# Converting 64-bit weights while the first tokens are computed: seven blocks' low parts through accumulating transfers, and a new order of the start

## The chip, the cores and the metric

The kernel runs on one core of a Trainium2 chip. The metric is the device time of one execution in microseconds (us). Three runs of the kernel before took 881.94, 882.14 and 883.23 us, median 882.14. The engines are named as the profile names them: PE (TensorE, matrix products; PEld is its loading of the fixed operand), DVE (VectorE), ACT (ScalarE), POOL (GpSimd) and SP (SyncE, which here only issues transfers).

## The reference, cut to what matters

Attention in chunks of 64 positions, then a normalised two-layer FFN with a residual:

```python
scores = 0.125 * q_chunk @ k_chunk.T            # 8 x 8 heads, 9 chunks of 64 x 64 each
attn = exp(scores - max(scores)); attn /= sum(attn) + 1e-9
x = (attn @ v_chunk)                            # heads side by side: 4608 tokens x 512
xn = (x - mean) / sqrt(var + 1e-6) * g_ln
out = x + relu(xn @ w_ch1) @ w_ch2              # 512 -> 2048 -> 512
```

q, k, v and g_ln are 32-bit floats. The two weight matrices come out of the set-up as 64-bit floats, since a 32-bit array is multiplied by a 64-bit scalar there, and the kernel takes them as they are.

## The kernel before

**Tiling.** The 4608 tokens are 18 pairs of 256 tokens (PAIR); two pairs make a tile of 512, so there are nine tiles. The hidden layer is cut into 16 blocks f of 128. For block f the FFN does an *up* product (512 to 128, line 369) into a PSUM tile h, a *rectification* (`split`, lines 377 and 378: ACT writes the high part hh, DVE the rest hl) and *down* products (128 to 512, line 389) that accumulate in the sums y. Every operand is kept as a high part and a rest ("low part"), both in the format F32R, and each product is three matmuls: high x high, high x low, low x high. With three matmuls for each of four k-slices, an up product is 12 matmuls; the down products of one block are 6 matmuls for a single pair and 12 for a tile.

**Attention of one pair** (`attention`): load q_t and k_t (one buffer each), scores on PE (line 206), maximum and subtraction on DVE (213, 219), load v_t, exponential on ACT (223), transposition of the probabilities, product with v on PE (271), division by the row sums (x, line 286 or 294), statistics (304), xg (309), transposition of xg and its splitting into xth and xtl. For the first four pairs (by_pe) both transpositions are done by PE against an identity (231, 321), and the rest xtl is made by PE too: the product of xth with minus the identity (328) is added to the transposed x in PSUM. For the first two pairs (den_by_pe) the row sums are PE products as well (275). All these PE transpositions, the scores and x of these pairs use one PSUM tile of two banks, `banks()`, of which there is one. The later pairs are transposed on DVE (242, 339).

**Conversion of the weights** (`convert_w`). There are 17 units: units 0 and 1 are the two halves of block 0 (512 columns each), unit i from 2 on is block i - 1 (1024 columns: 512 of w1, 512 of w2). A unit goes through these steps: *fetch* (SP, line 104) of the 64-bit words into raw, *start* (ACT, 112: absolute value of the upper words into wf), *round* (DVE, 119, 120, 123: clamp, shift, merge with the lower words; the result is written over the lower words inside raw, at a stride of 8 bytes), *sign* (DVE, 129, in place; then ACT, 133, casts the result to the high part wh), *split* (the low part wl = value - wh). The split of units 0 to 3 (BY_PE = 4) is two matmuls on PE in the first sum bank of pair 1 or its neighbour (144, 145: identity x value minus wh), copied out by ACT (146); that of the others is a DVE subtraction (148). There is one buffer wf and there are three for raw; two of these lie where later blocks' weights will stand.

**Order.** Nothing is ordered by a planner: the program is emitted under `tc.manual_schedule()`, and each engine and each queue takes its instructions in the order in which they are emitted. `play` walks a string; each letter advances one generator to its next `yield`. In START, a, b, A, B and E are the attention of pairs 0, 1, 2, 3 and 4, w the conversion, u and v the products of pairs 0 and 1 for the blocks 0 to 5 (SINGLE = 6), 1 and 2 their rectifications, y and 3 products and rectifications of the whole tile 0 for the blocks 6 to 15. STEADY is played seven times, for tiles 1 to 7, and LAST for tile 8. In a step of w that starts unit i + 1, the split of unit i - 1 and the fetch of unit i + 2 are emitted too.

Of the kernel before, what the change touches and what calls it, by code (L numbers as in the profile page):

```python
# [23 lines left out]
NPAIR = T // PAIR  # L24
NTILE = NPAIR // 2
HP = H // 2
NK = DM // P
NF = DFF // P
NW = 2 * DM
# [2 lines left out]

START = "aawwwwaawwwwwwawbwawwawbwbabwwaawaaawwbwwuA1wbbu1uwuwuAuB1Awubu1u1Awbwuu1bbbbuwvwAvw22AwAAvvvvB2EwA2wvv2vABvy2w3yBvwAww3vAyAwwywwyw3yA3BwyBwByByByBw3wB3wyByBww3yyBwwyEw3wywyy33yy3"
STEADY = "ABu1Au1AuAu1AuAu1AuABuAu1AEu1AuAu1AuAu1AuAu1BuBu1BuBu1BuBu1BuBEuBBu1BBu1BuBBu1Buu1uu1"
LAST = "u1u1uu1uu1uu1uu1uu1uu1uu1uu1uu1uu1uu1uu1uu1uu1u1"

SINGLE = 6

BY_PE = 4

ROOM = (3, 11)

# [9 lines left out]
def chunk_attention_ffn(ctx: ExitStack, tc: tile.TileContext, qkv, g, w, out):  # L54
    nc = tc.nc
    PSUM = bass.MemoryType.PSUM

    const = ctx.enter_context(tc.tile_pool(name="const", bufs=1))
# [6 lines left out]
    raws = ctx.enter_context(tc.tile_pool(name="raws", bufs=1))  # L65
# [4 lines left out]
    ident = const.tile([P, P], F32, name="ident")  # L70
    make_identity(nc, ident)
    minus = const.tile([P, P], F32R, name="minus")
    nc.scalar.activation(minus, ident, AF.Copy, scale=-1.0)
    ones = const.tile([P, 2], F32, name="ones")
    nc.gpsimd.memset(ones, 1.0)
    mhalf = const.tile([P, 2], F32, name="mhalf")
# [8 lines left out]
    def weights(f):  # L85
        if f not in wp:
            wp[f] = const.tile([P, 2, NW], F32R, name="wp", tag=f"w{f}")
        return wp[f][:, 0, :], wp[f][:, 1, :]

    def part(i):  # L90

        return (0, slice(i * HALF, (i + 1) * HALF)) if i < 2 else (i - 1, slice(0, NW))

    units = NF + 1
    stage, converted = {}, set()

    def fetch_w(i):
        if i < units:
# [6 lines left out]
            words = raw.bitcast(U32).rearrange("p (n two) -> p n two", two=2)  # L105
            stage[i] = words[:, :, 0], words[:, :, 1]

    def start_w(i):
        if i < units:
            lo, hi = stage[i]  # L110
            wf = raws.tile([P, NW], F32, name="wf")[:, : lo.shape[1]]
            nc.scalar.activation(wf, hi.bitcast(F32), AF.Abs)  # L112
            stage[i] = lo, hi, wf

    def round_w(i):

        lo, hi, wf = stage[i]
        wu = wf.bitcast(U32)
        nc.vector.tensor_scalar(out=wf, in0=wf, scalar1=F64_LOW, scalar2=F64_HIGH, op0=ALU.max, op1=ALU.min)
        nc.vector.tensor_scalar(  # L120
            out=wu, in0=wu, scalar1=0x07FFFFFF, scalar2=3, op0=ALU.bitwise_and, op1=ALU.logical_shift_left
        )
        nc.vector.scalar_tensor_tensor(  # L123
            out=lo, in0=lo, scalar=29, in1=wu, op0=ALU.logical_shift_right, op1=ALU.bitwise_or
        )

    def sign_w(i):
        lo, hi, _ = stage[i]
        nc.vector.scalar_tensor_tensor(
            out=lo, in0=hi, scalar=0xC0000000, in1=lo, op0=ALU.bitwise_and, op1=ALU.bitwise_or  # L130
        )
        f, cs = part(i)
        nc.scalar.copy(weights(f)[0][:, cs], lo.bitcast(F32))

    def split_w(i):
        wf = stage.pop(i)[0].bitcast(F32)
        f, cs = part(i)
        wh, wl = (x[:, cs] for x in weights(f))
        if i < BY_PE:
            for j in range(wf.shape[1] // HALF):  # L140
                js = slice(j * HALF, (j + 1) * HALF)
                assert 1 not in taken
                z = sums(1)[j % 2]
                nc.tensor.matmul(z, lhsT=ident, rhs=wf[:, js], start=True, stop=False)  # L144
                nc.tensor.matmul(z, lhsT=minus, rhs=wh[:, js], start=False, stop=True)
                nc.scalar.copy(wl[:, js], z)
        else:
            nc.vector.tensor_tensor(out=wl, in0=wf, in1=wh.bitcast(F32), op=ALU.subtract)
        converted.update((0, i) if i < 2 else (2 * i - 2, 2 * i - 1))

    def convert_w():

        fetch_w(0)
        yield
        start_w(0)
        for i in range(1, 4):
            fetch_w(i)
            yield
        for i in range(units):
            round_w(i)  # L160
# [12 lines left out]
    ys, taken = {}, set()

    def sums(pair):

        if pair not in ys:
            ys[pair] = [ps_y.tile([P, DM], F32, name="y") for _ in range(2)]
        return ys[pair]

    def attention(pair, xt_cols, xs, by_pe, den_by_pe):
# [7 lines left out]
        scale = 1.0 / float(D) ** 0.5  # L189
        groups = 2 * HP  # L190

        def banks():
            return ps_a.tile([P, 2, DM], F32, name="s")

        def rows(bank):
            return bank.rearrange("p (a d) -> p a d", d=D)

        s2 = banks()
        s = [rows(s2[:, h2, :]) for h2 in range(2)]
        for j in range(2):  # L200
            for a in range(HP):
                for h2 in range(2):
                    r = slice(h2 * D, (h2 + 1) * D)
                    for c in range(2):
                        cs = slice(j * P + c * D, j * P + (c + 1) * D)
# [20 lines left out]

        pt_sb = work.tile([P, groups, 2, D], F32, name="pt_sb", tag="work")
        if by_pe:
            pt = banks().rearrange("p j (a t) -> p j a t", a=HP)
            for a in range(groups):  # L230
                nc.tensor.transpose(out=pt[:, a // HP, a % HP, :], in_=p_sb[:, a, :, :], identity=ident)  # L231
            for j in range(2):
                nc.scalar.copy(
                    pt_sb[:, j * HP : (j + 1) * HP], pt[:, j].rearrange("p a (c t) -> p a c t", c=2)
                )
            yield
        else:
            for h2 in range(2):
                for j in range(2):
                    for c in range(2):  # L240
                        for i in range(2):
                            nc.vector.transpose(  # L242
                                out=pt_sb[quad(2 * h2 + j), :, c, quad(i)], in_=p_sb[quad(2 * c + i), :, h2, quad(j)]
                            )
                    yield
# [67 lines left out]

        xth, xtl = xt_cols()
        if by_pe:
            xt = banks()
            for j in range(2):
                js = slice(j * P, (j + 1) * P)
                for k in range(NK):
                    ks = slice(k * P, (k + 1) * P)  # L320
                    nc.tensor.matmul(  # L321
                        xt[:, j, ks], lhsT=xg[:, j, ks], rhs=ident, is_transpose=True, start=k == 0, stop=k == NK - 1
                    )
                nc.scalar.copy(xth[:, :, js], xt[:, j, :].rearrange("p (k t) -> p k t", k=NK))  # L324
                yield
            for j in range(2):
                js = slice(j * P, (j + 1) * P)
                nc.tensor.matmul(  # L328
                    xt[:, j, :], lhsT=minus, rhs=xth[:, :, js], start=False, stop=True, skip_group_check=True
                )  # L330
                nc.scalar.copy(xtl[:, :, js], xt[:, j, :].rearrange("p (k t) -> p k t", k=NK))  # L331
                if j == 0:
                    yield
        else:
            xt = work.tile([P, 2 * NK, P], F32, name="xt", tag="work")
            xg = xg.rearrange("p j (k t) -> p (j k) t", k=NK)
            for j in range(4):
                for i in range(4):
                    nc.vector.transpose(out=xt[quad(j), :, quad(i)], in_=xg[quad(i), :, quad(j)])  # L339
                yield  # L340
            for j in range(2):
                js = slice(j * P, (j + 1) * P)
                xt_j = xt[:, j * NK : (j + 1) * NK, :]
                nc.scalar.copy(xth[:, :, js], xt_j)  # L344
                nc.gpsimd.tensor_tensor(out=xtl[:, :, js], in0=xt_j, in1=xth[:, :, js].bitcast(F32), op=ALU.subtract)  # L345
# [7 lines left out]
    def ffn(pairs, xt, xs, f0, f1, room=()):  # L353
# [1 line left out]
        nt = len(pairs) * PAIR  # L355
        slots = DM // nt
        hs, held = {}, []
        tail = pairs[-1] == NPAIR - 1

        def up(f):  # L360
            assert 2 * f in converted and all(pair in xs for pair in pairs)
# [81 lines left out]
    def play(order, streams):  # L443
        for c in order:
            next(streams[c])
# [3 lines left out]
    class Tokens:  # L449
# [18 lines left out]
    now = {  # L468
        "a": tiles[0].attention(0, True, True), "b": tiles[0].attention(1, True, True),
        "A": tiles[1].attention(0, True), "B": tiles[1].attention(1, True),  # L470
        "E": tiles[2].attention(0), "w": convert_w(),
    }
    now.update(zip("u1", tiles[0].ffn(0, 1, 0, SINGLE)))
    now.update(zip("v2", tiles[0].ffn(1, 1, 0, SINGLE)))
    now.update(zip("y3", tiles[0].ffn(0, 2, SINGLE, NF)))
    with tc.manual_schedule():
        play(START, now)
        for t in range(1, NTILE):
            now.update(zip("u1", tiles[t].ffn(0, 2, room=ROOM if t + 1 < NTILE else ())))
            if t + 1 < NTILE:  # L480
                now.update(A=now.pop("E"), B=tiles[t + 1].attention(1))
            now["E"] = tiles[t + 2].attention(0) if t + 2 < NTILE else iter("  ")
            play(STEADY if t + 1 < NTILE else LAST, now)
# [33 lines left out]
```

## Time and profile before

The profiled execution took 884.8 us; its span, the part that the trace covers, is 883.0 us.

| | busy us | share of the span | instructions |
|---|---|---|---|
| PE | 856.3 | 97% | 6050 |
| PEld | 706.4 | 80% | 6050 |
| DVE | 538.3 | 61% | 963 |
| ACT | 173.6 | 20% | 262 |
| POOL | 50.6 | 6% | 54 |

Matmuls are pipelined and their recorded ends are modelled, so the duration of one matmul is longer than the distance to the next: an up product of a whole tile takes 2.72 us in the chain of waits, 12 matmuls at a distance of 0.227 us. In a row of instructions stand the start, the duration, the engine, the line of the kernel, the operation, what it writes and reads, its shape, and in brackets for how long the engine had been idle and what ended that. In a row of a group stand the count, then the sum and the mean (ns), then the idle time ahead. The first string's part of the execution ends at about 151 us: the outputs of tile 0 are issued from 150.81 us on.

### The profile page before, as it was taken

What the parts mean: (1) busy time and instruction counts of PE and PEld (TensorE: products, weight loads), DVE (VectorE), ACT (ScalarE), POOL (GpSimd) and SP (SyncE); (2) the same over time, 40 slices, a digit from 0 to 9 for tenths busy, and PEclk for the clock granted to TensorE, in tenths of its full rate; (3) what the DMA queues carried; (4) which work ended last, traced back from release to release, by engine and by line L of the source; (5) the groups of instructions that cost most, each with busy time, mean ns of one, the idle gap of its engine ahead of it and who ended that gap; (6) DMA issues with size and microseconds to landing.
All of it is one profiled execution on the core that took longest, in us unless ns stands there. A gap on an engine that the chain in (4) does not pass through costs nothing.

```text
span 883.0 us, 13918 instructions
## 1 busy us (share of the span) xinstructions
PE 856.3 (97%) x6050; PEld 706.4 (80%) x6050; DVE 538.3 (61%) x963; ACT 173.6 (20%) x262; POOL 50.6 (6%) x54
## 2 busy tenths in 40 slices
PE   4699999999999999999999999999999999999998
PEld 3378788888888888888888888888888888888886
DVE  5988885657575666567656766666566657661112
ACT  4543541111111211021112120212120111111110
POOL 0000000010100110010101010101010101010000
PEclk9799999999999999999999999999999999999999
DMA  7554241310032003200320032003200210010001
GB/s 298 206 201 168 95 144 49 104 39 1 1 120 72 1 1 119 73 1 1 119 73 1 1 120 73 1 1 120 73 1 1 79 66 0 1 48 1 1 1 48
DMA packets 18205, 55.67 MB, mean 63 GB/s; under 512 B 2017, under 2 KB 2017, under 8 KB 16225
## 3 DMA queue, kind: packets, MB, share of 16 engines
q1 hardware_dynamic: 18000, 54.53, 17.4%
q8 instruction: 47, 0.77, 0.4%
q10 hardware_dynamic: 144, 0.26, 0.1%
q14 instruction: 14, 0.11, 0.0%
HBM read 45.35 MB, written 9.44 MB: 62 GB/s over the span
## 4 chain that ended last, share of the span: by engine, by line
PE 97%; DVE 1%; issue 1%; ACT 1%; DMA 1%; SPq 0%
PE y L389 45%; PE h L369 45%; PE s L206 2%; PE h L271 2%; PE s L231 1%; DMA k_t<-qkv 1%; PE y L144 1%; PE s L271 1%; PE s L321 0%; PE s L328 0%; ACT xtl L331 0%; ACT xth L324 0%; PE y L275 0%; DVE raw L123 0%; DVE top L213 0%
## 5 line engine op out<-in xcount | busy, mean ns | idle before, releaser
L369 PE MATMUL h<-xth,wp 128*128 128x512 f32 (+1 forms) x1200 | 379.3, 382 | 0.0
L389 PE MATMUL y<-wp,hh 128*128 128x512 f32 x1152 | 358.1, 392 | 0.0
L378 DVE SCALAR_TENSOR_TENSOR hl<-h,hh 128x512 fp32r<-128x512 f32 (+1 forms) x150 | 100.4, 669 | 285.5 <-ACT hh L377 285.0
L369 PEld LDWEIGHTS h<-xth,wp 128*128 128x128 f32 x1200 | 224.0, 189 | 43.5
L389 PEld LDWEIGHTS y<-wp,hh 128*128 128x128 f32 x1152 | 214.8, 188 | 44.7 <-ACT hh L377 0.2
L369 PE MATMUL h<-xtl,wp 128*128 128x512 f32 (+1 forms) x600 | 228.9, 381 | 0.0
L389 PE MATMUL y<-wp,hl 128*128 128x512 f32 x576 | 224.9, 390 | 0.0
L377 ACT ACTIVATE hh<-h 128x512 fp32r<-128x512 f32 (+1 forms) x150 | 87.1, 580 | 575.8 <-PE h L369 556.3
L369 PEld LDWEIGHTS h<-xtl,wp 128*128 128x128 f32 x600 | 113.3, 189 | 21.9
L389 PEld LDWEIGHTS y<-wp,hl 128*128 128x128 f32 x576 | 108.4, 188 | 23.2 <-DVE hl L378 0.4
L339 DVE STREAM_TRANSPOSE xt<-xg 32x256 f32<-32x256 f32 x224 | 97.7, 436 | 3.7
L242 DVE STREAM_TRANSPOSE pt_sb<-p_sb 32x256 f32<-32x256 f32 x224 | 97.6, 436 | 3.1
L345 POOL TENSOR_TENSOR xtl<-xt,xth 128x512 fp32r<-128x512 f32 x28 | 35.6, 1292 | 609.4 <-ACT xth L344 609.4
L397 DVE SCALAR_TENSOR_TENSOR x<-y,rstd,x 128x512 f32<-128x512 f32 x36 | 25.3, 750 | 18.4 <-PE y L389 18.4
L206 PE MATMUL s<-k_t,q_t 64*64 64x64 f32 x1152 | 21.3, 224 | 7.9 <-DMA k_t<-qkv 6.8
L213 DVE TENSOR_REDUCE top<-s 128x16 f32<-128x1024 f32 x18 | 21.9, 1216 | 9.6 <-PE s L206 9.6
L223 ACT ACTIVATE p_sb<-p_sb 128x1024 f32<-128x1024 f32 x18 | 19.1, 1061 | 44.0 <-DVE p_sb L219 44.0
L206 PEld LDWEIGHTS s<-k_t,q_t 64*64 64x64 f32 x1152 | 19.4, 140 | 9.4 <-issue 9.2
L294 DVE TENSOR_TENSOR x<-h,rden 128x512 f32<-128x512 f32 x28 | 18.0, 686 | 12.1 <-PE h L271 12.1
L309 DVE SCALAR_TENSOR_TENSOR xg<-x,mv,g_sb 128x512 f32<-128x512 f32 x36 | 25.3, 743 | 0.0
L304 DVE BATCH_NORM_STATS2 stats<-x 128x6 f32<-128x512 f32 x36 | 24.3, 675 | 0.3
L112 ACT ACTIVATE wf<-raw 128x1024 f32<-128x1024 f32 (+1 forms) x17 | 18.7, 1100 | 21.7 <-DMA raw<-w 13.1
(47 smaller groups left out, 306.5 us busy)
## 6 DMA issues: line engine op xcount, KB each, us to landing
raw<-w SPq DMA_DIRECT2D x15, 1024.0 KB, 4.8
q_t<-qkv SPq DMA_DIRECT2D x18, 512.0 KB, 4.6
k_t<-qkv SPq DMA_DIRECT2D x18, 512.0 KB, 5.5
v_t<-qkv SPq DMA_DIRECT2D x36, 256.0 KB, 4.9
out<-x SPq DMA_DIRECT2D x36, 256.0 KB, 2.1
raw<-w SPq DMA_DIRECT2D x2, 512.0 KB, 6.7
g_sb<-g ACTq DMA_DIRECT2D x1, 256.0 KB, 4.8
```

Of the source, the lines that this page charges most:

```text
L206: nc.tensor.matmul(s[h2][c * D : (c + 1) * D, j * HP + a, :], lhsT=q_t[r, a, cs], rhs=k_t[r, a, cs], start=True, stop=True,)
L242: nc.vector.transpose(out=pt_sb[quad(2 * h2 + j), :, c, quad(i)], in_=p_sb[quad(2 * c + i), :, h2, quad(j)])
L271: nc.tensor.matmul(rows(o[h2])[cs, ja, :], lhsT=lhsT, rhs=v_t[j][r, a, c, :], start=True, stop=True)
L304: nc.vector.bn_stats(out=stats, in_=x[:, j, :])
L309: nc.vector.scalar_tensor_tensor(out=xg[:, j, :], in0=x[:, j, :], scalar=mv[:, j, 0:1], in1=g_sb, op0=ALU.subtract, op1=ALU.mult)
L339: nc.vector.transpose(out=xt[quad(j), :, quad(i)], in_=xg[quad(i), :, quad(j)])
L345: nc.gpsimd.tensor_tensor(out=xtl[:, :, js], in0=xt_j, in1=xth[:, :, js].bitcast(F32), op=ALU.subtract)
L369: nc.tensor.matmul(h, lhsT=wx, rhs=x[:, k, :], start=m == 0, stop=m == 3 * NK - 1)
L377: nc.scalar.activation(hh, h, AF.Relu)
L378: nc.vector.scalar_tensor_tensor(out=hl, in0=h, scalar=0.0, in1=hh.bitcast(F32), op0=ALU.max, op1=ALU.subtract)
L389: nc.tensor.matmul(sums(pairs[j // 2])[j % 2], lhsT=hx, rhs=wx, start=f == 0 and m == 0, stop=f == NF - 1 and m == 2,)
L397: nc.vector.scalar_tensor_tensor(out=x[:, jj, :], in0=sums(pair)[jj], scalar=rstd[:, jj : jj + 1], in1=x[:, jj, :], op0=ALU.mult, op1=ALU.add,
```

## The change

1. The split of units 4 to 10 (BY_DMA) is no longer a DVE subtraction. ACT writes the negated high part into wl after its cast, and a transfer issued by POOL adds the value from wf to it, with the addition done by the transfer.
2. BY_PE goes from 4 to 2: units 2 and 3 are now split by DVE.
3. Units 0 to 11 are "dense": the merge and the sign write into wf (contiguous) instead of into raw, and cast and split read wf. There are three such buffers in turn: the old one for i divisible by 3, and two that lie in the place of block 13's weights. raw is thus free after the sign step, and wf after the split.
4. For pairs 0 and 1 the transpositions by PE go into the two sum banks of the pair (each its own tile) instead of into the shared two-bank tile.
5. A new stream k: each step emits eight matmuls of minus the identity with itself, 128 columns, into the first sum bank of pair 0. Nothing reads the result. START has 14 of them. `minus` is made first, ahead of the first string.
6. START is written anew. Its letters are the same, in number too, apart from the 14 k. STEADY and LAST are unchanged. `tail` compares with 2 * NTILE - 1 in place of NPAIR - 1, which is the same number.

```diff
-START = "aawwwwaawwwwwwawbwawwawbwbabwwaawaaawwbwwuA1wbbu1uwuwuAuB1Awubu1u1Awbwuu1bbbbuwvwAvw22AwAAvvvvB2EwA2wvv2vABvy2w3yBvwAww3vAyAwwywwyw3yA3BwyBwByByByBw3wB3wyByBww3yyBwwyEw3wywyy33yy3"
+START = "kkkkwwakwbwkwawwwkwwkakkkaawbwwabbwbwaawbakbabbabawaubkAbukwB1AA1bbuwuAwv12wuAwvwv2wAvvvu2wwu2Av1vwAwuwAw21uvwBuwvv21BuwyvwBAw3wAyywuw3wAyww3yAwwAwy3BwyBBwByBBwyBy33wBwwEyy3wwwwyBywyy3wyBy33Eyy3"
-BY_PE = 4
+BY_PE = 2
+BY_DMA = (4, 5, 6, 7, 8, 9, 10)
+WARM = 8
...
-    nc.scalar.activation(minus, ident, AF.Copy, scale=-1.0)
...
+    def dense(i):
+        return part(i)[0] < NF - 5
+
     def start_w(i):
         if i < units:
             lo, hi = stage[i]
-            wf = raws.tile([P, NW], F32, name="wf")[:, : lo.shape[1]]
+            if not spare:
+                spare.append(const.tile([P, 2, NW], F32, name="wfs", tag=f"w{NF - 3}"))
+            if dense(i) and i % 3:
+                wf = spare[0][:, i % 3 - 1, : lo.shape[1]]
+            else:
+                wf = raws.tile([P, NW], F32, name="wf")[:, : lo.shape[1]]
             nc.scalar.activation(wf, hi.bitcast(F32), AF.Abs)
...
         nc.vector.scalar_tensor_tensor(
-            out=lo, in0=lo, scalar=29, in1=wu, op0=ALU.logical_shift_right, op1=ALU.bitwise_or
+            out=wu if dense(i) else lo, in0=lo, scalar=29, in1=wu, op0=ALU.logical_shift_right, op1=ALU.bitwise_or
         )
...
     def sign_w(i):
-        lo, hi, _ = stage[i]
+        lo, hi, wf = stage[i]
+        wu = wf.bitcast(U32) if dense(i) else lo
         nc.vector.scalar_tensor_tensor(
-            out=lo, in0=hi, scalar=0xC0000000, in1=lo, op0=ALU.bitwise_and, op1=ALU.bitwise_or
+            out=wu, in0=hi, scalar=0xC0000000, in1=wu, op0=ALU.bitwise_and, op1=ALU.bitwise_or
         )
         f, cs = part(i)
-        nc.scalar.copy(weights(f)[0][:, cs], lo.bitcast(F32))
+        wh, wl = (x[:, cs] for x in weights(f))
+        stage[i] = wu.bitcast(F32)
+        nc.scalar.copy(wh, stage[i])
+        if i in BY_DMA:
+            nc.scalar.activation(wl, wh.bitcast(F32), AF.Copy, scale=-1.0)
...
+        elif i in BY_DMA:
+            nc.gpsimd.dma_start(wl, wf, accum_op=ALU.add)
         else:
             nc.vector.tensor_tensor(out=wl, in0=wf, in1=wh.bitcast(F32), op=ALU.subtract)
...
+    def keep_warm():
+        while True:
+            assert 0 not in taken
+            for i in range(WARM):
+                nc.tensor.matmul(sums(0)[0][:, :P], lhsT=minus, rhs=minus, start=True, stop=True)
+            yield
...
+        def halves():
+            if den_by_pe:
+                assert pair not in taken
+                return sums(pair)
+            both = banks()
+            return [both[:, j, :] for j in range(2)]
...
-            pt = banks().rearrange("p j (a t) -> p j a t", a=HP)
+            pt = halves()
...
-            xt = banks()
+            xt = halves()
+            if den_by_pe:
+                taken.add(pair)
...
     with tc.manual_schedule():
+        nc.scalar.activation(minus, ident, AF.Copy, scale=-1.0)
         play(START, now)
```

More of the change, by code (lines that the diff above doesn't have):

```diff
@@ L30 @@
 HALF = NW // 2
-START = "aawwwwaawwwwwwawbwawwawbwbabwwaawaaawwbwwuA1wbbu1uwuwuAuB1Awubu1u1Awbwuu1bbbbuwvwAvw22AwAAvvvvB2EwA2wvv2vABvy2w3yBvwAww3vAyAwwywwyw3yA3BwyBwByByByBw3wB3wyByBww3yyBwwyEw3wywyy33yy3"
+START = "kkkkwwakwbwkwawwwkwwkakkkaawbwwabbwbwaawbakabbabawaubkAbukwB1AA1bbuwuAwv12wuAwvwv2wAvvvu2wwu2Av1vwAwuwAw21uvwBuwvv21BuwyvwBAw3wAyywuw3wAyww3yAwwAwy3BwyBBwByBBwyBy33wBwwEyy3wwwwyBywyy3wyBy33Eyy3"
 STEADY = "ABu1Au1AuAu1AuAu1AuABuAu1AEu1AuAu1AuAu1AuAu1BuBu1BuBu1BuBu1BuBEuBBu1BBu1BuBBu1Buu1uu1"
@@ L94, in chunk_attention_ffn @@
     units = NF + 1
-    stage, converted = {}, set()
+    stage, converted, spare = {}, set(), []
     def fetch_w(i):
@@ L123, in round_w @@
         nc.vector.scalar_tensor_tensor(
-            out=lo, in0=lo, scalar=29, in1=wu, op0=ALU.logical_shift_right, op1=ALU.bitwise_or
+            out=wu if dense(i) else lo, in0=lo, scalar=29, in1=wu, op0=ALU.logical_shift_right, op1=ALU.bitwise_or
         )
     def sign_w(i):
-        lo, hi, _ = stage[i]
+        lo, hi, wf = stage[i]
+        wu = wf.bitcast(U32) if dense(i) else lo
         nc.vector.scalar_tensor_tensor(
-            out=lo, in0=hi, scalar=0xC0000000, in1=lo, op0=ALU.bitwise_and, op1=ALU.bitwise_or
+            out=wu, in0=hi, scalar=0xC0000000, in1=wu, op0=ALU.bitwise_and, op1=ALU.bitwise_or
         )
         f, cs = part(i)
-        nc.scalar.copy(weights(f)[0][:, cs], lo.bitcast(F32))
+        wh, wl = (x[:, cs] for x in weights(f))
[3 more added lines that the diff above has]
+            nc.scalar.activation(wl, wh.bitcast(F32), AF.Copy, scale=-1.0)
     def split_w(i):
-        wf = stage.pop(i)[0].bitcast(F32)
+        wf = stage.pop(i)
         f, cs = part(i)
@@ L228, in attention @@
         if by_pe:
-            pt = banks().rearrange("p j (a t) -> p j a t", a=HP)
+            pt = halves()
             for a in range(groups):
-                nc.tensor.transpose(out=pt[:, a // HP, a % HP, :], in_=p_sb[:, a, :, :], identity=ident)
+                cs = slice(a % HP * P, (a % HP + 1) * P)
+                nc.tensor.transpose(out=pt[a // HP][:, cs], in_=p_sb[:, a, :, :], identity=ident)
             for j in range(2):
                 nc.scalar.copy(
-                    pt_sb[:, j * HP : (j + 1) * HP], pt[:, j].rearrange("p a (c t) -> p a c t", c=2)
+                    pt_sb[:, j * HP : (j + 1) * HP], pt[j].rearrange("p (a c t) -> p a c t", a=HP, c=2)
                 )
@@ L321, in attention @@
                     nc.tensor.matmul(
-                        xt[:, j, ks], lhsT=xg[:, j, ks], rhs=ident, is_transpose=True, start=k == 0, stop=k == NK - 1
+                        xt[j][:, ks], lhsT=xg[:, j, ks], rhs=ident, is_transpose=True, start=k == 0, stop=k == NK - 1
                     )
-                nc.scalar.copy(xth[:, :, js], xt[:, j, :].rearrange("p (k t) -> p k t", k=NK))
+                nc.scalar.copy(xth[:, :, js], xt[j].rearrange("p (k t) -> p k t", k=NK))
                 yield
@@ L328, in attention @@
                 nc.tensor.matmul(
-                    xt[:, j, :], lhsT=minus, rhs=xth[:, :, js], start=False, stop=True, skip_group_check=True
+                    xt[j], lhsT=minus, rhs=xth[:, :, js], start=False, stop=True, skip_group_check=True
                 )
-                nc.scalar.copy(xtl[:, :, js], xt[:, j, :].rearrange("p (k t) -> p k t", k=NK))
+                nc.scalar.copy(xtl[:, :, js], xt[j].rearrange("p (k t) -> p k t", k=NK))
                 if j == 0:
                     yield
+            if den_by_pe:
+                taken.remove(pair)
         else:
@@ L357, in ffn @@
         hs, held = {}, []
-        tail = pairs[-1] == NPAIR - 1
+        tail = pairs[-1] == 2 * NTILE - 1
         def up(f):
@@ L470, in chunk_attention_ffn @@
         "A": tiles[1].attention(0, True), "B": tiles[1].attention(1, True),
-        "E": tiles[2].attention(0), "w": convert_w(),
+        "E": tiles[2].attention(0), "w": convert_w(), "k": keep_warm(),
     }
```

## The prediction

> **What bounds the kernel now.** I read the page's table of slices first, then busy time by stage, then the chain of work that ended last, then PE's and VectorE's instructions of the first 45 us in order of time.
>
> ```profile
> 0.00:8.80 8.80, 1.99 (x64) 1.83 (x64) 0.00 (x0) 2.13 (x3) 0.77 (x8) 1.00 0.81 292
> 20.00:33.70 13.70, 7.98 (x173) 4.55 (x167) 13.04 (x20) 6.95 (x9) 0.00 (x0) 0.95 0.77 270
> 33.70:41.90 8.20, 5.39 (x19) 3.58 (x19) 7.10 (x9) 5.63 (x9) 1.21 (x1) 0.50 0.22 60
> 41.90:48.80 6.90, 6.90 (x155) 6.66 (x154) 4.97 (x9) 3.58 (x5) 0.00 (x0) 0.71 0.67 255
> 62.70:69.80 7.10, 5.07 (x18) 3.62 (x18) 6.40 (x10) 4.80 (x8) 1.60 (x1) 0.76 0.20 55
> 69.80:108.00 38.20, 38.18 (x327) 32.81 (x325) 33.00 (x44) 16.48 (x24) 0.00 (x0) 1.00 0.40 142
> 150.70:793.00 642.30, 642.30 (x4428) 531.91 (x4427) 407.82 (x788) 97.02 (x154) 44.66 (x42) 1.00 0.13 46
> ```
>
> After the length of a stage stand the busy us of PE, PEld, DVE, ACT and POOL, then the granted clock. From 150.7 to 793 PE is busy for 642.30 of 642.30 us: nothing outside the first order string can move the time, unless its length does. All the slack of PE lies before 70 us, and there VectorE is nearly full (13.04 of 13.70). The clock is 0.50 from 33.7 to 41.9 and 0.76 from 62.7 to 69.8, the two places where one pair's x is transposed.
>
> ```profile
> 42.24 2.56 PE h L369 x12
> 48.96 1.39 PE y L389 x6
> 53.16 1.09 PE s L206 x64
> 60.08 1.43 PE h L369 x12
> 62.90 0.45 PE s L321 x4
> 67.30 2.56 PE y L389 x6
> 99.58 2.73 PE h L369 x12
> ```
>
> ```profile
> 11.24 0.42 DVE L119 TENSOR_SCALAR wf<-wf 128x512 f32<-128x512 f32 x1
> 15.27 0.70 DVE L129 SCALAR_TENSOR_TENSOR raw<-raw 128x512 uint32<-128x512 uint32 x1
> 16.49 0.69 DVE L119 TENSOR_SCALAR wf<-wf 128x1024 f32<-128x1024 f32 x1 [0.52 <-ACT wf L112]
> 19.21 1.23 DVE L129 SCALAR_TENSOR_TENSOR raw<-raw 128x1024 uint32<-128x1024 uint32 x1
> 23.05 0.23 DVE L281 TENSOR_SCALAR den<-y 128x8 f32<-128x8 f32 x2
> 24.75 1.22 DVE L129 SCALAR_TENSOR_TENSOR raw<-raw 128x1024 uint32<-128x1024 uint32 x1
> 27.47 0.68 DVE L304 BATCH_NORM_STATS2 stats<-x 128x6 f32<-128x512 f32 x1
> 29.09 1.19 DVE L219 TENSOR_TENSOR p_sb<-s,top 128x1024 f32<-128x1024 f32 x1
> ```
>
> ```profile
> 33.67 1.09 PE L321 MATMUL s<-ident,xg 128*128 128x128 f32 x4 [4.33 <-DVE xg L309]
> 38.80 0.80 PE L328 MATMUL s<-xth,minus 128*128 128x512 f32 x1 [0.68 <-ACT xtl L331]
> 41.89 0.56 PE L369 MATMUL h<-xth,wp 128*128 128x256 f32 x1
> 108.66 1.09 PE L231 MATMUL s<-ident,p_sb 128*128 128x128 f32 x8 [0.68 <-ACT xtl L331]
> ```
>
> So the front reads: VectorE reaches pair 0's xg late (33.67), a serial PE-ACT chain at half clock follows to 41.89, the first down product starts at about 48.8 (48.96 in the chain), and pair 1's transposition costs a second gap. A step of the chain at half clock takes 2.56 us, at full clock 1.43 (up) or 1.39 (down).
>
> **The change part by part.** Both strings run the same steps of attention, conversion and FFN; the new one adds fourteen k. I add up from the start to four points.
>
> *To pair 0's first transposition.* The new order fetches weight unit 0 ahead of q and k. The rows: SP's first issue, the chain's first piece, the landing times of q_t in the first 20 us (the first was the 4.6), and groups by form.
>
> ```profile
> 0.74 0.37 SPq L186 DMA_DIRECT2D q_t<-qkv  x1
> 1.16 5.50 DMA k_t<-qkv
> DMA to landing us min/median/max: 4.6/6.3/8.0
> L112 ACT ACTIVATE wf<-raw 128x512 f32<-128x512 f32 x2 | 1.4, 688 | 6.0 <-DMA raw<-w 5.5 <-DVE raw L123 0.5
> L324 ACT CAST xth<-s 128x512 fp32r<-128x512 f32 x8 | 4.7, 586 | 1.7 <-PE s L321 1.5
> L309 DVE SCALAR_TENSOR_TENSOR xg<-x,mv,g_sb 128x512 f32<-128x512 f32 x36 | 25.3, 743 | 0.0
> L148 DVE TENSOR_TENSOR wp<-raw,wp 128x1024 fp32r<-128x1024 f32 x13 | 15.8, 1214 | 1.9 <-ACT wp L133 1.9
> ```
>
> The first 512 KB landed at 0.74 + 4.6 = 5.3, the second at 6.66, 1.3 later. Unit 0 takes the first place: 5.3, plus 0.7 for its absolute value, so VectorE begins at 6.0. Rounding and signing units 0 and 1 took from 11.24 to 15.97, 4.7: done at 10.7. Pair 0's k is now fourth: 6.66 + 2 x 1.3 = 9.3, and its scores at the old 2.0 (the first stage's busy PE) end at 11.3. Maximum and subtraction 2.4: 13.7. Unit 2 is rounded (16.49 to 19.21, 2.7) and signed (1.2): 17.6. Pair 1's q and k are issued on SP behind pair 0's scores, since q_t and k_t have one buffer each, and unit 3's fetch and pair 0's v queue behind that wait: 11.3 + 0.4 + 5.5 = 17.2, scores 1.4 (between 2.0 and the chain's 1.09), 18.6; maximum and subtraction, 21.0. Then unit 3's rounding 2.6, unit 2's subtraction 1.2 (PE did it before), den and x 1.7 (23.05 to 24.75), statistics 1.6 (27.47 to 29.09), sign 1.2, half of xg 0.7: **30.0 against 33.67**. Pair 0's v should land at 17.2 + 2.6 + 1.3 = 21.1 and its product is wanted at 24.8; these 3.7 us less the product's own time are the cover, and beyond it each us of late loading is a us of all that follows. PE's removed products of units 2 and 3 lay in PE's idle time and bring nothing.
>
> *To the first up product.* Each half now has its own bank, so the second half's transposition no longer waits for the first half's copy, and pair 1's probabilities are transposed earlier. At half clock: 1.1 twice for PE, 0.6 for the copy, 0.8 twice, 0.6: 30.0 + 4.4 = **34.4 against 41.89**.
>
> *To the first down product.* Up 2.6, transpositions of pair 1 2 x 0.6, up 1.6, scores of A 1.1, two low parts 0.8, two k at about 0.5 (eight matmuls of 128 columns, between a quarter of the 0.80 row and the same at full clock): 34.4 + 8.3 = **42.7 against 48.8**. VectorE's x, statistics and xg of pair 1 end at 30.7 + 1.7 + 1.6 + 1.3 = 35.3, rounding, subtraction and first rectification at 39.5: no wait. Gain so far 6.1.
>
> *After it.* Moved ahead of this point are A's scores (1.1) and pair 1's chain, 62.7 to 67.1 (4.4), with the down product behind it at half clock (2.56 - 1.39 = 1.2); the 0.68 us at 108.66 goes too, since pair 2 is transposed with more between. 7.3 us. VectorE keeps 12 roundings, 13 signs, 6 subtractions, two pairs' attention and 22 rectifications, about 81 us (12 x 2.6 + 13 x 1.2 + 6 x 1.2, twice 8 for attention, 22 times 0.4 to 0.7, a subtraction of L309's size), and PE 94 (12 downs at 1.39, 10 ups at 1.43, 20 of twice the columns at 2.73, and 8 for attention). VectorE must no longer do seven subtractions, 8.5 us. New waits cannot be read: none if VectorE never idles, and it idled some 5 in each 38 us (33.00 busy of 38.20 above), which would be 5. I take 3.
>
> *The accumulating transfer.* No row shows one, nor ACT's negation of a block (nearest: 1.15, below). Its ends, from the issues by line, raw's landings in the first 30 us, and groups by form:
>
> ```profile
> out<-x SPq DMA_DIRECT2D x36, 256.0 KB, 2.1
> raw<-w SPq DMA_DIRECT2D x15, 1024.0 KB, 4.8
> DMA to landing us min/median/max: 4.8/6.3/10.6
> L133 ACT CAST wp<-raw 128x1024 fp32r<-128x1024 f32 x15 | 17.2, 1148 | 9.0 <-DVE raw L129 8.9
> L112 ACT ACTIVATE wf<-raw 128x1024 f32<-128x1024 f32 x15 | 17.3, 1155 | 15.7 <-DVE raw L123 8.1 <-DMA raw<-w 7.6
> L123 DVE SCALAR_TENSOR_TENSOR raw<-raw,wf 128x1024 uint32<-128x1024 uint32 x15 | 18.4, 1227 | 0.6
> L120 DVE TENSOR_SCALAR wf<-wf 128x1024 uint32<-128x1024 uint32 x15 | 10.4, 694 | 0.5
> ```
>
> It reads 1 MB (source and target) and writes 0.5. Below 2.1 it cannot be, the longest 1 MB fetch in the crowded start took 10.6; I take that start's median, 6.3, and 1 for the issue on GpSimd: 7.3. By the sums above unit 4's negation is done at about 44 and its low part is wanted by an up product at 52, 8 us later; for the following units the distance is 7 to 9. But three conversion buffers turn: ACT's absolute value of unit i+3 waits for unit i's transfer, and behind it on ACT stand the rectifications that PE waits for. That distance is 6 to 8 us. So 7.3 is just at the edge: cost 1 us (0 at 2.1; about 6 at 11.6).
>
> The Trainium skill (DMA: Bandwidth & Descriptors, section "Anatomy of one DMA — SWDGE (gpsimd) path") puts a transfer issued by GpSimd at about 2.0 us plus bytes over 436 GB/s; my estimate from it is 3.2 us for 0.5 MB and 4.4 if the target's read counts, and the sum would then lose the 1 us. The same skill (SBUF — State Buffer, section "SBUF: two separate sides") says against this change that GpSimd cannot write descriptors while VectorE runs in a two-port mode. L120 does 1024 elements in 694 ns where L123 needs 1227, so such a mode is in use here; no run so far shows a blocked descriptor. By that rule two such instructions per unit hold an issue back by at most 1.4 us, some 1 us of the sum.
>
> ACT gains seven negations (8 us) and loses four copies; with 16.48 busy of 38.20 it has the room, unless it stands still at a buffer. Dense buffers change no VectorE duration by these rows: L148 (reads raw) and L123 take 1214 and 1227 for 1024 elements either way.
>
> **Sum:** -6.1 - 7.3 + 3 + 1 = -9.4 us. The profiled execution took 884.8 (span 883.0), 2.7 over the median; the same loss from the median gives 882.14 - 9.4 = 872.7, so 872.5.
>
> **The rivals.** (a) *The front runs as summed, losses of 0 to 7 later:* 866 to 876. Speaks for it: PE never waited from 70 us on in the old order although VectorE had more to do. (b) *VectorE and ACT wait in turns:* in the new order VectorE has no gap of its own from 21 to 60 us, so every late load, copy or half-clock product is handed on; the losses grow from 4 to 8 or 12: 876 to 880. Against it: 81 against 94 us. (c) *The buffer ring binds, and the kernel is slower.* One turn is absolute value 1.15, rounding 2.6, sign 1.2, cast 1.15, negation 1.15, together 7.3, plus the transfer, over three units. PE eats a unit in 5.5. The gain of 9.4 is used up when seven units take 1.35 more each, at (7.3 + L)/3 = 6.85, L = 13 us; from there it decides, and at L = 20 the kernel takes 882.14 - 9.4 + 7 x 3.6 = 898. For it: nothing here shows the arithmetic in a transfer; against: L would have to be above every landing shown. (d) *The k don't do what they are for:* PE stays at half clock from 20 to 45 us as it did; I have priced the chain to the first up at half clock already, so only the second up and what follows it, 3 us: 876. In that case the rest holds. (e) *The front gains more*, full clock throughout and no later waits: 860 to 866.
>
> **How the numbers follow.** (a) 0.50, (b) and (d) together 0.22, (e) 0.08, (c) 0.20, of which 0.14 slower than before by over 0.2%, 0.03 within it and 0.03 still faster. 0.2% (1.8 us) is about what a measurement of this kernel can tell from no change. A little of (b) may end within it as well: same 0.06, slower 0.14, faster 0.80. The likeliest case's own range is 866 to 876; 8 in 10 needs (b) and the near end of (c): 863 to 883.
>
> **What would show it.** Pair 0's first transposition (L321 before) near 30 us, the first up product near 34, the first down near 43, PE without a wait from 60 us on, and everything after the first string some 9 us earlier; PE clock above 0.5 before 45 us; no VectorE subtraction for units 4 to 10; ACT's wait ahead of an absolute value put down to the GpSimd transfer at under 2 us in total. Wrong would be a landing over 10 us, ACT idle ahead of absolute values for over 5 us, or PE idle after 60 us for more than 5.

## The result, and the profile after

The changed kernel takes 887.79 us (median of four runs, 885.90 to 889.79) against 882.11 us before: ratio 1.0062, 95% interval 1.0038 to 1.0087. It is slower by 0.6%; 872.5 was predicted. Its profiled execution, the quickest of the four, took 885.9 us with a span of 884.1, against 884.8 and 883.0 before.

The page of the changed kernel (span, busy times, the group of the warm-ups, transfers by line with their median landing):

```profile
span 884.1 us, 14121 instructions
PE 870.6 (98%) x6150; PEld 725.6 (82%) x6150; DVE 532.1 (60%) x958; ACT 177.1 (20%) x265; POOL 56.7 (6%) x61
L196 PE MATMUL y<-minus 128*128 128x128 f32 x112 | 21.3, 369 | 2.8 <-ACT minus L516 2.8
wp<-wfs POOLq DMA_DIRECT2D x5, 512.0 KB, 7.5
wp<-wf POOLq DMA_DIRECT2D x2, 512.0 KB, 5.0
L123 ACT ACTIVATE wfs<-raw 128x1024 f32<-128x1024 f32 x7 | 8.0, 1144 | 7.8 <-DMA wp<-wfs 5.2 <-DMA raw<-w 2.6
```

PE is busier by 14.3 us and VectorE less by 6.2. The warm-ups alone are 21.3 us of PE. The last row, from the list of groups by form, is ACT's absolute values (L123): they waited 5.2 us for transfers, in two waits. The same stages as in the prediction (busy PE, PEld, DVE, ACT, POOL, then the granted clock):

```profile
0.00:8.80 8.80, 5.97 (x28) 5.97 (x29) 2.45 (x5) 3.13 (x5) 0.77 (x8) 1.00 0.77 286
8.80:20.00 11.20, 11.20 (x102) 9.84 (x101) 6.51 (x9) 2.15 (x4) 0.00 (x0) 1.00 0.51 171
33.70:41.90 8.20, 8.14 (x146) 7.37 (x142) 7.96 (x17) 2.78 (x5) 0.00 (x0) 0.50 0.85 348
62.70:69.80 7.10, 4.53 (x24) 3.90 (x24) 2.87 (x6) 1.41 (x2) 0.64 (x1) 0.86 0.91 252
```

From 8.8 to 20 us PE is full and VectorE is not: the front has changed hands. The column shows clock 1.00 there, but the scores, 1.09 us at full clock, take 1.92 below; in these traces the column can't be used until 20 us, and I go by durations. The chain that ended last in the changed kernel (start, us, what):

```profile
2.83 10.51 PE y L196 x48
13.33 1.92 PE s L240 x64
15.25 1.90 PE y L196 x8
...
19.39 3.91 PE y L196 x32
23.30 0.89 PE y L266 x8
...
37.07 1.90 PE y L196 x8
...
46.41 1.36 PE y L196 x8
...
49.67 0.84 PE y L196 x8
...
56.93 10.27 DMA wp<-wfs
```

All fourteen k stand in it, 20.4 us together: six ahead of pair 0's scores (L240), five ahead of the transposition of its probabilities (L266), one ahead of its first transposition of xg, two behind. Then comes the first accumulating transfer. PE's order of time (start, duration) gives the points that the prediction used, the first product that waited for a transfer, and that wait:

```profile
38.77 1.93 PE L358 MATMUL y<-ident,xg 128*128 128x128 f32 x8
41.96 0.42 PE L408 MATMUL h<-xth,wp 128*128 128x256 f32 x1
52.10 0.63 PE L428 MATMUL y<-wp,hh 128*128 128x512 f32 x2
67.25 0.51 PE L408 MATMUL h<-xth,wp 128*128 128x256 f32 x2 [2.57 <-DMA wp<-wfs]
```

### The profile page after: what moved, and what is told of

Same layout as the page of the kernel before. It is cut to its first block, busy times and chain, and to the rows that moved or that the text cites. A ratio compares the mean times of both kernels' runs of the same rounds, so it can differ in the third digit from the quotient of the medians.

```text
span 884.1 us, 14121 instructions
## 1 busy us (share of the span) xinstructions
PE 870.6 (98%) x6150; PEld 725.6 (82%) x6150; DVE 532.1 (60%) x958; ACT 177.1 (20%) x265; POOL 56.7 (6%) x61
## 4 chain that ended last, share of the span: by engine, by line
PE 96%; DVE 2%; DMA 1%; ACT 0%; issue 0%; ACTq 0%; DVEq 0%
PE h L408 44%; PE y L428 44%; PE y L196 2%; PE s L240 2%; PE h L306 2%; DMA wp<-wfs 1%; PE s L306 0%; PE y L358 0%; DVE top L247 0%; DVE p_sb L253 0%; PE y L160 0%; PE s L358 0%; PE y L310 0%; ACT L516 0%; DVE x L321 0%; DVE wf L134 0%
## 5 line engine op out<-in xcount | busy, mean ns | idle before, releaser
L416 ACT ACTIVATE hh<-h 128x512 fp32r<-128x512 f32 (+1 forms) x150 | 86.4, 579 | 562.3 <-PE h L408 542.6
L196 PE MATMUL y<-minus 128*128 128x128 f32 x112 | 21.3, 369 | 2.8 <-ACT minus L516 2.8
L196 PEld LDWEIGHTS y<-minus 128*128 128x128 f32 x112 | 20.8, 286 | 3.6 <-ACT minus L516 2.8
L383 ACT CAST xth<-xt 128x512 fp32r<-128x512 f32 x28 | 16.0, 618 | 31.5 <-DVE xt L378 31.5
```

Source lines behind the costliest of these rows:

```text
L196: nc.tensor.matmul(sums(0)[0][:, :P], lhsT=minus, rhs=minus, start=True, stop=True)
L416: nc.scalar.activation(hh, h, AF.Relu)
```

## The experiments

Theory W: the warm-ups hold PE's queue and with it the whole front. Rivals: T, the transfers behind the turn of three buffers; O, the new order itself; C, the warm-ups pay for themselves by the clock.

**Take one thing away each** (e1 to e4). In the new START, as it was run, the letters after `waawbak` are `abbaba`; the diff under "The change" has one b too many there.

```diff
-START = "kkkkwwakwbwkwawwwkwwkakkkaawbwwabbwbwaawbakabbabawaubkAbukwB1AA1bbu...
+START = "wwawbwwawwwwwaaawbwwabbwbwaawbaabbabawaubAbuwB1AA1bbu...
```

> All fourteen k steps are taken out of the first string; nothing else. Theory W (the warm-ups delay the front): in the changed kernel 48 warm-up matmuls run from 2.83 to 13.3 us at 0.22 us each, and pair 0's scores, whose k should have landed at about 9.4, start only at 13.26. Without them the scores start at 9 to 10, pair 1's loads go out 4 us earlier, the first down product comes at 43 to 46 instead of 52.1, and the time is 878 to 882. Theory C (the warm-ups pay for themselves by the clock): PE stays at half clock longer, the front gets no shorter, 886 to 890. Theory T (the transfers cost): no change beyond 1 us, 886 to 889.

```diff
-BY_DMA = (4, 5, 6, 7, 8, 9, 10)
+BY_DMA = ()
```

> The low parts of units 4 to 10 are DVE subtractions again (no negation on ACT, no transfer); order, warm-ups and dense buffers as in the changed kernel. Theory T (the accumulating transfers cost the time: the first landed after 10.3 us and PE stood 2.6 us and then ran at lower clock): 881 to 884. Theory W (warm-ups): DVE gets 8.5 us of work back between 56 and 105 us, in a stretch where it is nearly full, and PE's wait for the transfer turns into waits for DVE: 887 to 893.

```diff
-START = "kkkkwwakwbwkwawwwkwwkakkk...
+START = "aawwwwaawwwwwwawbwawwawbw...
```

> The changed kernel with the first string of before (no k in it): transfers, dense buffers, two units by PE and the single banks stay. Theory W and theory O (the new order itself costs the time) both expect the front of before: first down product at 47 to 50 us, 880 to 884. If the transfers cost (theory T), 885 or more, with ACT idle ahead of absolute values behind a transfer.

```diff
-            nc.gpsimd.dma_start(wl, wf, accum_op=ALU.add)
+            nc.gpsimd.dma_start(wl, wf)
```

> The seven transfers copy the value into the low part instead of adding it (the low parts are then wrong; everything else is the same). If the arithmetic in the transfer costs, the landings fall from a median of 7.5 and 5.0 us to those of a load of the same size, 2 to 4 us, and the wait of PE behind the first one goes. If the queue costs (the transfer stands among loads of 1 MB), the landings stay within 1 us of 7.5 and the first stays near 10.

| | median us | before, same chip | ratio, 95% interval |
|---|---|---|---|
| e1, no k | 873.89 | 882.65 | 0.9902 (0.9877 to 0.9926) |
| e2, no transfers | 890.13 | 882.65 | 1.0084 (1.0068 to 1.0101) |
| e3, order of before | 890.62 | 882.65 | 1.0083 (1.0065 to 1.0100) |
| e4, plain copies, one run | 885.97 | 882.65 | |

e1 settles most: without the k the kernel is 13.9 us faster than with them and 8.8 faster than before, more than theory W had asked (878 to 882); the time lies in none of the three ranges. PE's order of time in e1:

```profile
9.50 1.99 PE L240 MATMUL s<-k_t,q_t 64*64 64x64 f32 x64 [9.50 <-DMA k_t<-qkv]
16.07 1.09 PE L266 MATMUL y<-ident,p_sb 128*128 128x128 f32 x8 [2.15 <-ACT p_sb L257]
17.09 1.92 PE L240 MATMUL s<-k_t,q_t 64*64 64x64 f32 x64
30.60 1.97 PE L358 MATMUL y<-ident,xg 128*128 128x128 f32 x8
33.83 0.41 PE L408 MATMUL h<-xth,wp 128*128 128x256 f32 x1
40.19 0.62 PE L428 MATMUL y<-wp,hh 128*128 128x512 f32 x2
```

The scores wait for the load alone, and pair 0's probabilities are transposed at 16.1 instead of 23.3. Theory C falls by the time itself. The clock is mixed: the changed kernel ran pair 0's scores at half clock after 10.5 us of warm-ups, as e1 did without any (1.99 each). e1 then has the full clock for the transposition at 16.07 (1.09) and has lost it again for pair 1's scores (1.92 at 17.09), which the changed kernel ran at full clock (1.16), but seven us later, at 24.13.

e2 speaks against theory T for this order: without the transfers the median is 2.3 us higher, not lower, though the two intervals overlap; theory W had 887 to 893. Its first down product came at 55.78, 3.7 later than in the changed kernel's trace, which no transfer explains, as the changed kernel's first one starts at 56.93; from there to the start of tile 1 the two take the same, 100.37 and 100.74 us. In its chain VectorE's work stands where the transfer stood, a subtraction (L166) among it, and PE waits 1.9 us for VectorE's rectifications instead of 2.6 for a transfer:

```profile
60.60 1.23 DVE wfs L134
61.83 0.66 DVE hl L417 x2
62.49 1.13 DVE wp L166
```

e3 surprised me: I had the order of before, with no warm-up in it, at 880 to 884, and it is as slow as anything here. Its chain of waits names the transfers:

```profile
38.92 12.03 DMA wp<-wfs
...
50.97 1.12 ACT wfs L123
52.09 0.28 ACT hh L416
...
56.42 8.06 DMA wp<-wf
```

The next absolute value (L123) starts when the transfer has landed and its buffer is free, and the rectification (L416) that PE waits for stands behind it on ACT. Over the whole trace ACT's absolute values waited 8.2 us for transfers:

```profile
L123 ACT ACTIVATE wfs<-raw 128x1024 f32<-128x1024 f32 x7 | 8.0, 1139 | 8.6 <-DMA wp<-wfs 8.2 <-DMA raw<-w 0.3
```

e4 leaves out the addition. Its transfers land after medians of 5.1 and 3.8 us:

```profile
wp<-wfs POOLq DMA_DIRECT2D x5, 512.0 KB, 5.1
wp<-wf POOLq DMA_DIRECT2D x2, 512.0 KB, 3.8
```

Against the changed kernel's 7.5 and 5.0 the addition costs 2.4 and 1.2 us a landing, in between the two expectations. The size rests on one pair of traces: in the others the medians of the sums go from 5.7 to 8.5 and from 5.0 to 8.9, all above the copies. In e4's execution the first down product came at 56.45, 4.3 later than in the changed kernel's trace, because the same 32 warm-ups took 6.92 us and not 4.12, and tile 1 began at the same time (152.90 against 152.84). That the shorter landings gave these 4 us back is not shown: e9 below, with sums and a late front too (52.48), has no wait of PE for a transfer either and takes 97.2 us from there to tile 1, e4 96.5, the changed kernel 100.7.

**Cross the factors, and change the warm-ups' shape** (e5 to e8).

e5 is e1 and e2 together, e7 is e2 and e3 together:

```diff
-START = "kkkkwwakwbwkwawwwkwwkakkk...
+START = "wwawbwwawwwwwaaawbwwabbwb...
-BY_DMA = (4, 5, 6, 7, 8, 9, 10)
+BY_DMA = ()
```

> The new order without warm-ups and without transfers: units 4 to 10 subtracted by DVE. Against the kernel without warm-ups (873.9) it tells what the transfers bring when the front is not held up; there the chain of waits runs through three transfers (6.99, 6.73 and 9.96 us). If the turn of three buffers behind the transfers is the bound, the time is 870 to 874; if DVE is the bound, as the sum of the prediction has it (8.5 us more on DVE), 876 to 882.

```diff
-START = "kkkkwwakwbwkwawwwkwwkakkk...
+START = "aawwwwaawwwwwwawbwawwawbw...
-BY_DMA = (4, 5, 6, 7, 8, 9, 10)
+BY_DMA = ()
```

> First string of before, with dense buffers, two units by PE and single banks, but DVE subtracts units 4 to 10. With transfers this order took 890.6. If the transfers behind the turn of three buffers made that slow (12.0 and 8.1 us in its chain of waits), the time falls to 880 to 884. If two more units on DVE or the single banks made it slow, it stays at 888 to 893.

```diff
+    wide = minus.rearrange("p (one c) -> p one c", one=1).broadcast_to([P, DM // P, P])
-WARM = 8
+WARM = 2
-                nc.tensor.matmul(sums(0)[0][:, :P], lhsT=minus, rhs=minus, start=True, stop=True)
+                nc.tensor.matmul(sums(0)[0], lhsT=minus, rhs=wide, start=True, stop=True)
```

> Each k is two matmuls of 512 columns instead of eight of 128: the same columns, a quarter of the weight loads. Theory L (a warm-up of 128 columns costs its weight load, 0.22 us each, twice what its columns need, and a PE that is half empty in this way is not granted the full clock): a k falls from 1.75 to about 0.9 us, PE's first scores run at 1.1 to 1.2 us instead of 1.9 and start by 10 us, and the time is 872 to 878. Theory P (any work of PE ahead of the scores costs, and the clock comes or not by other causes): the scores still take 1.9 us, 876 to 882.

```diff
-START = "kkkkwwakwbwkwawwwkwwkakkk...
+START = "kkkkwwawbwwawwwwwaaa...
```

> Only the first four k stay (32 matmuls of 128 columns from 2.83 us on, ending at about 9.9 by 0.22 us each); the ten others go. Theory W: they end 0.4 us after pair 0's k has landed, so this costs 0.4 to 1 us against the kernel without warm-ups: 874 to 876. If the first warm-ups bring the clock up, scores in 1.2 us instead of 2.0 and 871 to 873. If the k between the scores and the first down product were not the cost, but these four are: 880 or more.

| | median us | before, same chip | ratio, 95% interval |
|---|---|---|---|
| e5, no k, no transfers | 875.10 | 882.61 | 0.9912 (0.9897 to 0.9926) |
| e6, fourteen dense k | 871.58 | 882.61 | 0.9865 (0.9847 to 0.9884) |
| e7, order of before, no transfers | 879.89 | 882.61 | 0.9965 (0.9951 to 0.9979) |
| e8, the first four k | 872.52 | 882.61 | 0.9878 (0.9864 to 0.9893) |

Now the parts can be told apart. Dense buffers, single banks and two units by PE together, in the order of before: -2.7 us (e7, whose 879.89 lies at the edge of the 880 to 884 expected if the transfers made e3 slow). The new order on top of them: -4.8 (e7 to e5). The transfers: -1.2 in the new order (e5 to e1, where the intervals overlap: a small gain or nothing; e5's 875.1 lies between the two ranges expected), but +10.7 in the order of before (e7 to e3). The fourteen warm-ups: +13.9 (e1 to the changed kernel).

The loss in the order of before is the prediction's buffer ring. e3's chain shows ACT at the next absolute value before the buffer is free, and it waited 8.2 us for transfers, where e7's absolute values into `wfs` waited 0.1 in all. From the first down product to tile 1, e3 takes 108.3 us and e7 100.6; PE waited 2.6 us for the rectification and 1.9 for a transfer, and its granted clock over the stretch was 0.97 against 1.00. In e1 ACT waited as long for transfers (6.7 and 1.5 us), but PE only 2.6, so it is what stands behind the absolute values that decides. e1's chain runs through the transfers too:

```profile
45.24 6.99 DMA wp<-wfs
...
57.73 6.73 DMA wp<-wf
...
70.32 9.96 DMA wp<-wfs
```

That fits e8, whose front is later than e1's and whose time is not longer (1.4 us less, intervals overlapping): the first down product at 43.06 instead of 40.19, but tile 1 begun at 139.44 instead of 140.06. What e1's front gains over e8's it waits for later: the 2.6 us on PE, which e8 does not have. e8's PE order:

```profile
2.83 7.09 PE L196 MATMUL y<-minus 128*128 128x128 f32 x32 [2.83 <-ACT minus L516]
9.85 1.99 PE L240 MATMUL s<-k_t,q_t 64*64 64x64 f32 x64
```

Four k push the scores back by 0.35 us (9.85 against 9.50 in e1): as good as free, and no help, since the scores still take 1.99. The time falls into the range expected of warm-ups that bring the clock up (871 to 873), but not for that reason. In e6 (the kernel has one line more, so 196 is 197) a warm-up has four times the columns:

```profile
L197 PE MATMUL y<-minus 128*128 128x512 f32 x28 | 10.3, 509 | 2.8 <-ACT minus L517 2.8
2.84 4.50 PE L197 MATMUL y<-minus 128*128 128x512 f32 x12 [2.84 <-ACT minus L517]
9.45 1.99 PE L241 MATMUL s<-k_t,q_t 64*64 64x64 f32 x64 [2.11 <-DMA k_t<-qkv]
17.07 1.16 PE L241 MATMUL s<-k_t,q_t 64*64 64x64 f32 x64
```

Six k take 4.50 us instead of 10.5 and end before the load; all fourteen are 10.3 us of PE instead of 21.3. Theory L of that expectation was right on the price, and the time (871.58) lies just below its 872 to 878; on the first scores it was not, in this execution (1.99).

**Which k, and a better version** (e9 to e12). e9 keeps the first eleven k:

```diff
-START = "kkkkwwakwbwkwawwwkwwkakkkaawbwwabbwbwaawbakabbabawaubkAbukwB1...
+START = "kkkkwwakwbwkwawwwkwwkakkkaawbwwabbwbwaawbaabbabawaubAbuwB1...
```

> The changed kernel without its last three k, those between pair 0's xg and the first down product (1.90 + 1.36 + 0.84 = 4.1 us in the changed kernel's chain). Fourteen k cost 13.9 us against none, the first four nothing. If each k costs its own time on PE where PE is on the chain, the last three cost 4 us: 883 to 885. If the seven in the middle, which stand between pair 0's scores and both pairs' transpositions, hold the front up by themselves, 885 to 888. If the last three cost most, by keeping PE's weight loads in front of the first products, 876 to 881.

e10 is e1 with transfers for every second unit only:

```diff
-BY_DMA = (4, 5, 6, 7, 8, 9, 10)
+BY_DMA = (5, 7, 9)
```

> No k, and transfers only for units 5, 7 and 9; DVE subtracts 4, 6, 8 and 10 (4 x 1.2 = 4.9 us more for it). Without k, seven transfers gave 873.9 and none 875.1. If the turn of three buffers behind seven transfers is the bound (6.99, 6.73 and 9.96 us in the chain), every second transfer has a turn's time to land: 870 to 873. If DVE is the bound, the time lies between the two, 874 to 875.

e11 has the order of e9 and the wide warm-ups of e6 (`WARM = 2`, the second operand `wide`, all 512 columns):

```diff
-WARM = 8
+WARM = 2
-                nc.tensor.matmul(sums(0)[0][:, :P], lhsT=minus, rhs=minus, start=True, stop=True)
+                nc.tensor.matmul(sums(0)[0], lhsT=minus, rhs=wide, start=True, stop=True)
```

> Eleven k of two matmuls of 512 columns, the last three dropped; seven transfers. With all fourteen dense k the time was 871.6 and the last three took 1.15 + 0.55 + 0.55 us on PE's way to the first down product. If that is on the path, 869 to 870.5; if the time after the first down product is set by DVE and the transfers, 871 to 872.

e12 is e11 with the three transfers of e10:

```diff
-BY_DMA = (4, 5, 6, 7, 8, 9, 10)
+BY_DMA = (5, 7, 9)
```

> As the eleven dense k, with transfers for units 5, 7 and 9 only. If the buffers' turn still binds with the earlier front, 867 to 869.5; if DVE binds, 870 to 873, as much slower than with seven transfers as DVE's four subtractions show.

| | median us | before, same chip | ratio, 95% interval |
|---|---|---|---|
| e9, the first eleven k | 885.08 | 882.68 | 1.0008 (0.9980 to 1.0035) |
| e10, no k, three transfers | 872.83 | 882.68 | 0.9885 (0.9869 to 0.9901) |
| e11, eleven dense k | 869.56 | 882.68 | 0.9852 (0.9832 to 0.9871) |
| e12, the same, three transfers | 869.85 | 882.68 | 0.9854 (0.9836 to 0.9873) |

By the medians the last three k cost 2.7 us (887.79 to 885.08), the first four nothing (e8), so the seven in the middle cost 12.6. e9's ten runs spread over 13 us, and without the longest the median is 884.75, so this split is rough; that the middle seven cost most is clear. e9's PE order shows how:

```profile
2.83 10.50 PE L196 MATMUL y<-minus 128*128 128x128 f32 x48 [2.83 <-ACT minus L516]
13.27 1.99 PE L240 MATMUL s<-k_t,q_t 64*64 64x64 f32 x64
15.18 1.97 PE L196 MATMUL y<-minus 128*128 128x128 f32 x8
16.95 2.02 PE L160 MATMUL y<-wf,ident 128*128 128x512 f32 x2
17.97 1.42 PE L161 MATMUL y<-wp,minus 128*128 128x512 f32 x1
19.19 6.92 PE L196 MATMUL y<-minus 128*128 128x128 f32 x32
25.91 1.93 PE L266 MATMUL y<-ident,p_sb 128*128 128x128 f32 x8
```

From 2.83 to 25.9 PE has no gap. k steps five and six push the scores from 9.85 to 13.27; the seventh and four more stand ahead of the transposition of the probabilities, which comes at 25.91 (e8: 16.42), 9.5 us late, and so does all behind it.

Transfers for every second unit are neither clearly better nor worse than for all seven: e10 is 1.1 us below e1, e12 0.3 above e11, all within the intervals. e10's 872.83 lies in the range of the ring (870 to 873), e12's 869.85 between its two ranges; neither the ring nor VectorE is shown to bind in the new order. e11's 869.56 lies in the range for the last three k on the path, 2.0 below e6, but those two intervals overlap as well. e11 has the lowest median here, 13.1 us below before and 18.2 below the changed kernel; e12, e6 and e8 lie within 3 us of it with intervals that overlap. Its PE order, lines one later than in the changed kernel:

```profile
2.83 5.25 PE L197 MATMUL y<-minus 128*128 128x512 f32 x12 [2.83 <-ACT minus L517]
9.53 1.16 PE L241 MATMUL s<-k_t,q_t 64*64 64x64 f32 x64 [1.45 <-DMA k_t<-qkv]
15.04 1.09 PE L267 MATMUL y<-ident,p_sb 128*128 128x128 f32 x8 [0.77 <-ACT p_sb L258]
```

## Why the prediction was wrong

| step | forecast | changed kernel | e1, no k |
|---|---|---|---|
| pair 0's scores begin | 9.3 | 13.26 | 9.50 |
| pair 0's first transposition of xg | 30.0 | 38.77 | 30.60 |
| first up product | 34.4 | 41.96 | 33.83 |
| first down product | 42.7 | 52.10 | 40.19 |
| new waits after it, a remainder | 4 | 5.1 | 4.3 |
| median | 872.5 | 887.79 | 873.89 |

(New waits: the shift of the first down product against before's 48.79, plus the 7.3 us moved or removed, less the change of the span from 883.0: -3.3 + 7.3 + 1.1 for the changed kernel, 8.6 + 7.3 - 11.6 for e1. They are what is left over, not waits that were measured.)

**The step that failed is the one to pair 0's first transposition.** Its sum has a term for every instruction of VectorE and none for the twelve k emitted ahead of that point; only the two later ones were priced, at 0.5 us each. It came at 38.77 instead of 30.0, and at 30.60 in e1. I had named no work that hides the twelve. The wait for the first load hides four (e8) and no more: in these traces PE takes its queue in order, so a warm-up emitted ahead of the scores runs ahead of them whether or not the load has landed (by 9.5 in e1; the scores began at 13.26), and one emitted ahead of a transposition delays it.

The price of the two was wrong too. A step of eight took 1.75 to 1.97 us at half clock and 0.84 at full. The 0.5 does not even follow from the row it names: a quarter of 0.80 is 0.20 for one matmul of 128 columns, so 1.6 for eight, and 0.8 at full clock, both near what was measured (48 of them took 10.51 us, 0.219 each). Priced by columns, they are dear: twelve matmuls of 512 columns took 4.50 to 5.25 us, 0.375 to 0.44 each, so of two equal stretches of columns the one cut into 128s costs about twice as much. That the weight load sets this floor (mean PEld of the warm-ups 286 ns) fits, but was only argued.

**What held, and what was luck.** That nothing outside the first string moves the time: from the start of tile 1 to the end took 731.1 us before, 731.3 in the changed kernel and in e1. The sum without the k: e1's points lie within 0.6 us of the forecast up to the first up product, and its median 1.4 us above the forecast. Part of that is luck. The step to the first up product adds up to 5.0 us by its own terms, not the 4.4 written, and took 3.2 in both kernels, which made up for a first transposition 0.6 late. The first down product came 2.5 earlier in e1, of which 1 us is the two k priced there. And the traces are other executions than the medians: before's is 2.7 us above its median, e1's 0.8 below, so of the 11.6 us between the two traces only 8.8 stand in the medians, and the remainders in the table are uncertain by as much. What can be read directly: from the first down product to tile 1 PE waited 3.3 us both in the changed kernel and in e1 (2.6 for transfers, 0.7 for ACT's copies) and 0.7 in e8. That stretch took 103.2 us before and 96.4 in e8, so 6.8 of the 7.3 us are there; the changed kernel took 100.7, since behind its wait the clock was lower too (0.86 from 62.7 to 69.8).

The landing was taken as 7.3 with the issue: medians 7.5 and 5.0, the first 10.27 from the start of its issue. POOL's instruction that issues one took 0.87 to 1.35 us, near the 1 assumed; whether VectorE ever held a descriptor back is shown by no run. By the Trainium skill's formula (DMA: Bandwidth & Descriptors, "Anatomy of one DMA — SWDGE (gpsimd) path") my estimate was 3.2 us for half a MB and 4.4 with the target's read; in this crowded start the measurement is above it for copies (3.8 and 5.1) and sums (5.0 and 7.5) alike.

**The signs of being wrong.** Two of the three showed: a landing over 10 us (10.27) and ACT waiting over 5 us for transfers (5.2, where under 2 was forecast). PE waited less than 5 us behind the front. But e1 has the same two signs (longest landing 10.3 us, 8.2 us of waiting) and is 8.8 us faster than before, so they point at the ring and not at the step that failed.

**The rivals.** (d), that the k don't do what they are for, is in part what happened, but I had priced only the missing clock (876) and not the time of the warm-ups themselves. The Trainium skill (TensorE: Matmul & The Clock Gate, "Part 1: The HAM clock gate") has about 3.4 us of sustained activity bring the full clock. Here it did not: in e9 PE was without a gap from 2.83 to 25.9 us and the transposition at its end still took 1.93 us, against 1.09 at full clock; the measurement decides. (c), the buffer ring, forecast a slower kernel, but for a reason that is not the one found: in the new order the transfers cost nothing by the medians, and PE's wait for them is 2.6 us in the changed kernel and e1 and none in e6, e8, e9 and e11. The ring is real in e3, where with the order of before the transfers cost 10.7 us. Its point, L = 13 us, was set for a turn in the new order's pace; in e3 the chain shows 12.03 and 8.06 and the loss was there already. (a) describes e1.

## What to carry to other kernels

Price filler work in the queue where it stands: PE ran it here before whatever was emitted next, so it is free only as far as the next wait covers it (here four steps ended 0.35 us after the load, six 3.8), and price it from an instruction of its own width. An edit costed at nothing needs its cover named; the one missing from this sum cost 13.9 us, where the whole forecast gain was 9.4. A transfer that takes work from a busy engine can change sign with the order around it: the same seven gained 1.2 to 2.3 us by the medians in one order, which is not clear of the noise, and cost 10.7 in the other.

## What I had not expected of the hardware

Warm-up matmuls of 128 columns, with scores and splitting products between them and no gap for 23 us, did not bring PE to full clock in e9, while e1 had it for one transposition at 16.07 us with PE idle for a good part, and had lost it at 17.09. e11, with 512 columns, had it for its first scores at 9.53 us; e6 with the same form did not (1.99), had it at 17.07 (1.16), and its transposition at 25.03 took 1.97 again. What grants the clock so early in an execution stays open. The times spread with it: ten runs of e9 took from 876.95 to 890.23 us, where those of the kernel before, on the same chip, lay between 881.95 and 884.98. In the two traces the same 32 warm-ups took 6.92 us (e9) and 4.12 (the changed kernel), so the moment at which the clock comes moves by several us from one execution to the next; that this makes all of the spread is argued, since only one execution of each kernel was traced.
